# Spreading the second score product of a gated linear attention over four column quarters of TensorE

## Chip, core and metric

The kernel runs on one core of a Trainium2 chip. The metric is the device time of one launch in microseconds; the number given for a kernel is the median of its runs. Before the change it is 628.76 us (three runs, 627.93 to 629.44).

## What is computed

A gated recurrence over the sequence feeds a feed-forward block. For each of 4 batches and 8 heads (768 steps, 48 numbers per head) a complex state S is rotated and shrunk at each step by a gate (its size held below 0.999), takes up the outer product of k and v, and is read out by q:

```python
for t in range(S):
    ar, ai = a_re_n[:, :, t, :, None], a_im_n[:, :, t, :, None]
    new_re = ar * S_re - ai * S_im
    new_im = ar * S_im + ai * S_re
    S_re, S_im = new_re + einsum('bhd,bhe->bhde', k[:, :, t], v[:, :, t]), new_im
    y[:, :, t] = einsum('bhd,bhde->bhe', q[:, :, t], S_re)
x = y.transpose(0, 2, 1, 3).reshape(3072, 384)
h = maximum(maximum(x @ w1, x @ w2), x @ w3)        # 384 -> 768
out = h @ w_out                                      # 768 -> 384
```

All data are float32.

## The kernel before

**Tiles.** The sequence is cut into blocks of 128 steps. A group g is one block of two batches; each of its two halves (x and y in the step names, number x = 2g or 2g+1 in the code) is one block of one batch with 8 heads. There are 12 groups, so 24 halves. A block of 128 steps is two chunks of 64. Inside a chunk the recurrence is written as products: q and k are turned by the running angle of the gates and scaled by running products of their sizes, a masked score matrix (key step by query step) takes the place of the recurrence, and a state per head is carried from chunk to chunk.

**Scores.** In `scores` (L590) the step `A` (L602) multiplies K by Q for every head in pieces of 32 keys. Each product has 32 columns of weights, and its output lies in one of the four sets of 32 partitions (0, 32, 64, 96), which is one of the four column quarters of TensorE. In order, `A` walks over the four quarters for each head: 32 products a half, each with 80 columns of the moving operand. The steps `g0` to `g3` pick what is wanted out of A by masks into the tile `atm` (128 key steps, 8 heads, 64 query steps), on VectorE.

The second score product, step `B` (L608), covers the block of the first 32 keys against the last 32 queries of each chunk. It has a product for each head h and each chunk j: weights `KB` and moving operand `QB`, 32 columns each, 16 products a half. The output of chunk j lies at partition 64j, so the products use two of the four quarters, and column block h of one PSUM bank. Its results are carried to `atm` by `b0` and `b1` (L632), one ScalarE copy for each chunk: 32 partitions, 8 heads by 32 queries, from partitions 64j to the same partitions of `atm`. The step `y` (L678) then multiplies `v` and the carried state with `atm` and `QG`; its 56 products of 32 weight columns and 64 moving columns are spread over the four quarters by a round-robin over four queues.

**Feed-forward.** `xT` is a copy of y. The steps U (`up`, L710) make the three hidden products 128 by 128 by 256, u takes their maximum (`hT`), O and o make the output product (`op`) and its copy `ot`.

**What sets the order.** Every engine's order is written out by hand in two lists of step names: SCHEDULE (L21) for the opening, groups 0 and 1 and the preparation of the weights, and CYCLE (L52) for each later group. A small class (Bound, L122) ties each instruction to the one before it on its engine, so no scheduler moves anything; all instructions are issued from its line 131, so the profile shows L131 for all of them and they are told apart by the names of tiles. All PSUM tiles (`banks`, L141) rotate through four buffers of two banks each, so a fifth request waits until the first buffer has been read.

Each cycle of CYCLE has two B steps on TensorE: in one half the order is A, B, op, up, y, and in the other A, B, tp (a transpose of uq), op, y, tp.

Of the kernel before, what the change touches and what calls it, by code (L numbers as in the profile page):

```python
# [67 lines left out]
def kernel(  # L68
# [14 lines left out]
    B, H, S, D = q.shape  # L83
    P = 128
    L64 = 64
    DD = L64 + D
# [32 lines left out]
    T = {}  # L119
# [18 lines left out]
    pe, dve, act, pool, sp = (Bound(e) for e in (nc.tensor, nc.vector, nc.scalar, nc.gpsimd, nc.sync))  # L138
    mm = pe.matmul

    def banks(nm, n=None):  # L141

        ps = psum.tile([P, 2, 512], FP, tag="ps", name=nm)
        T["ps"] = ps
        return ps if n is None else ps.rearrange("p a n -> p (a n)")[:, 0:n]
# [61 lines left out]
    KB = const.tile([P, 2 * H, 32], FP, name="KB")  # L207
# [382 lines left out]
    def scores(x, name):  # L590

        atm = T["atm", x] = atms[x % 2]

        def pick(out, mask, data):
            dve.copy_predicated(out=out, mask=mask, data=data)

        def over(mask):

            n = mask.shape[-1]
            return mask.rearrange("p (b t) -> p b t", b=1).to_broadcast([P, H, n])  # L600

        if name == "A":  # L602
            ps = T["A", x] = banks("A")
            for h in range(H):
                for o in range(0, P, 32):
                    mm(out=ps[o:o + 32, h // HU, h % HU * P:h % HU * P + 80], lhsT=T["K", x][0:DD, h, o:o + 32],
                       rhs=T["Q", x][0:DD, 4 * h + o // 32], start=True, stop=True)
        elif name == "B":  # L608
            ps = T["B", x] = banks("B")
            for h in range(H):  # L610
                for j in range(2):
                    o = j * L64
                    mm(out=ps[o:o + 32, 0, h * 32:h * 32 + 32], lhsT=T["KB", x][0:DD, 2 * h + j],
                       rhs=T["QB", x][0:DD, 2 * h + j], start=True, stop=True)
        elif name[0] == "g" and name[1:].isdigit():
            src = T["A", x].rearrange("p a (b t) -> p (a b) t", b=HU)

            def own(lo, n):

                return src[:, :, lo:lo + n].rearrange("p h (j t) -> p h j t", j=1).to_broadcast([P, H, 2, n])  # L620

            i = int(name[1:])
            if i == 0:
                pick(atm.rearrange("p h (j t) -> p h j t", j=2), over(maskd).rearrange("p h (j t) -> p h j t", j=2),
                     own(0, 32))
            elif i == 1:
                pick(atm.rearrange("p h (j n u w) -> p h j n u w", j=2, n=2, u=2)[:, :, :, :, 1],
                     over(masko[:, 0]).rearrange("p h (j n w) -> p h j n w", j=2, n=2), own(48, 16))
            else:
                pick(atm.rearrange("p h (j u w) -> p h j u w", j=2, u=2)[:, :, :, 1],  # L630
                     over(masko[:, i - 1]).rearrange("p h (j w) -> p h j w", j=2), own(32 * (i - 1), 16))
        elif name in ("b0", "b1"):  # L632
            o = int(name[1]) * L64
            src = T["B", x][:, 0, 0:H * 32].rearrange("p (h t) -> p h t", h=H)
            act.copy(out=atm[o:o + 32, :, 32:], in_=src[o:o + 32])
        else:
            return False
        return True
# [106 lines left out]
    def run(name, g):  # L745
# [9 lines left out]
        elif name == "Zf":  # L755
            for t in fs:
                dve.memset(t[L64 // 2:L64], 0.0)
        elif name == "Zg":
            for t in gs:
                dve.memset(t[:, :, :, D:P - D], 0.0)  # L760
        elif name[0] == "W":
            i = int(name[2:])
            weight_load(i) if name[1] == "L" else weight_step(i, name[1])
        elif name[0] in "Uu" and name[1:].isdigit():
            up(2 * g + 1, TG, int(name[1]), int(name[2]), name[0].upper() if name[0] == "U" else "u")
        elif name[0] in "Uu" and name[1:3].isdigit():
            up(2 * g + "xy".index(name[3]), P, int(name[1]), int(name[2]), name[0])
        elif name[-1] in "01" and gates(g, [int(name[-1])], name[:-1]):
            pass
        elif gates(g, list(range(C)), name):  # L770
            pass
        else:
            c = "xy".index(name[-1])
            x, name = g * C + c, name[:-1]
            if name in ("Lr", "Li"):
                load_a(g, c, *(("ar", a_re) if name == "Lr" else ("ai", a_im)))
            elif name in ("Lk", "Lq"):
                load_kq(g, c, *(("k", k) if name == "Lk" else ("q", q)))
            elif name == "Lv":
                load_v(g, c)  # L780
            else:
                assert angles(g, c, name) or turns(g, c, name) or factors(x, name) or scores(x, name) \
                    or state(x, name) or outputs(x, name) or project(x, name), name
# [51 lines left out]
```

## Time and profile before

| what | before |
|---|---|
| median of runs | 628.76 us |
| the profiled execution's own time | 627.78 us |
| its span, first to last instruction | 625.9 us |
| mean granted TensorE clock | 0.986 |
| matmul instructions of B / A / y | 768 / 1536 / 2560 |
| ScalarE copies atm<-B | 48, 356 ns each |

A product of float32 is recorded as two weight loads and two matmuls, so the 16 products of one B step are 32 instructions of each kind. In the tables PE is TensorE's matmuls, PEld its weight loads, ACT ScalarE, DVE VectorE. "Busy" of PE counts matmuls that overlap in the array and whose ends are modelled; what a step costs is better read from where the next one starts. The chain of work gives the sequence of instructions that the end of the kernel depended on. An engine's idle time is noted with what released it.

### The profile page before, as it was taken

What the parts mean: (1) busy time and instruction counts of PE and PEld (TensorE: products, weight loads), DVE (VectorE), ACT (ScalarE), POOL (GpSimd) and SP (SyncE); (2) the same over time, 40 slices, a digit from 0 to 9 for tenths busy, and PEclk for the clock granted to TensorE, in tenths of its full rate; (3) what the DMA queues carried; (4) which work ended last, traced back from release to release, by engine and by line L of the source; (5) the groups of instructions that cost most, each with busy time, mean ns of one, the idle gap of its engine ahead of it and who ended that gap; (6) DMA issues with size and microseconds to landing.
All of it is one profiled execution on the core that took longest, in us unless ns stands there. A gap on an engine that the chain in (4) does not pass through costs nothing.

```text
span 625.9 us, 22651 instructions
## 1 busy us (share of the span) xinstructions
PE 588.8 (94%) x10124; PEld 473.1 (76%) x10124; DVE 478.7 (76%) x694; ACT 429.2 (69%) x698; POOL 14.3 (2%) x47
## 2 busy tenths in 40 slices
PE   4466899899999999999999999999999999999997
PEld 1255797688787787787788788788788788788785
DVE  6998999989887887877777787887887887754211
ACT  8998998795894894894894894894894893541100
POOL 3500000000000000000000000000000000000000
PEclk9976999999999999999999999999999999999999
DMA  9788411442222223122222222222230221000000
GB/s 241 171 210 209 115 20 35 93 80 43 50 57 51 51 56 72 27 60 52 50 56 52 53 54 52 53 52 52 53 66 15 41 53 28 15 3 15 15 13 25
DMA packets 136545, 39.24 MB, mean 63 GB/s; under 512 B 129153, under 2 KB 132225, under 8 KB 136449
## 3 DMA queue, kind: packets, MB, share of 16 engines
q1 hardware_dynamic: 136448, 37.80, 27.3%
q8 instruction: 79, 1.29, 0.9%
q14 instruction: 18, 0.14, 0.1%
HBM read 33.03 MB, written 4.72 MB: 60 GB/s over the span
## 4 chain that ended last, share of the span: by engine, by line
PE 84%; ACT 6%; DVE 5%; DMA 3%; issue 1%; SPq 1%; DVEq 0%; ACTq 0%
PE up L131 43%; PE op L131 16%; PE y L131 6%; PE A L131 4%; PE tp L131 4%; PE dk L131 3%; PE cs L131 2%; PE sums L131 2%; PE B L131 2%; DVE ex L131 2%; DVE w L131 2%; PE F L131 1%; DMA ai<-in_a_im_dram 1%; DMA raw<-in_moe_w_out_dram 1%; ACT L L131 1%
## 5 line engine op out<-in xcount | busy, mean ns | idle before, releaser
L131 PE MATMUL up<-xT,w 128*128 128x256 f32 (+1 forms) x1404 | 297.4, 368 | 2.2 <-ACT E L131 0.7
L131 PEld LDWEIGHTS up<-xT,w 128*128 128x128 f32 x1404 | 248.5, 191 | 39.8 <-ACT L L131 1.7
L131 DVE TENSOR_TENSOR hT<-hT,up 128x768 f32<-128x768 f32 (+1 forms) x56 | 46.8, 837 | 80.1 <-PE up L131 80.1
L131 PE MATMUL op<-wo,hT 128*128 128x384 f32 x288 | 98.8, 494 | 0.0
L131 PEld LDWEIGHTS op<-wo,hT 128*128 128x128 f32 x288 | 53.0, 190 | 33.4
L131 DVE TENSOR_TENSOR Q<-Q,f 112x512 f32<-112x512 f32 (+2 forms) x72 | 68.6, 953 | 9.6 <-ACT Q L131 9.2
L131 ACT ACT_TABLE_LOAD x47 | 60.3, 1283 | 1.6 <-PEq L819 0.8
L131 ACT COPY xT<-y 128x384 f32<-128x384 f32 x24 | 11.4, 476 | 62.6 <-PE y L131 62.6
L131 PE MATMUL y<-atm,vb 128*32 128x64 f32 x1152 | 39.9, 225 | 3.8 <-issue 3.0
L131 PEld LDWEIGHTS y<-atm,vb 128*32 128x32 f32 x1152 | 32.9, 112 | 13.7 <-issue 7.4
L131 ACT ACTIVATE f<-F 48x280 f32<-48x280 f32 x96 | 38.2, 398 | 2.5 <-PE F L131 1.2
L131 ACT ACTIVATE t<-cs 128x384 f32<-128x384 f32 x24 | 11.8, 491 | 39.8 <-PE cs L131 39.8
L131 PE MATMUL y<-QG,g 112*32 112x64 f32 x1408 | 38.8, 221 | 0.0
L131 PE MATMUL A<-Q,K 112*32 112x80 f32 x1536 | 32.6, 239 | 3.1 <-ACT w L131 2.6
L131 PEld LDWEIGHTS y<-QG,g 112*32 112x32 f32 x1408 | 35.3, 111 | 0.3 <-DVE g L131 0.2
L131 PEld LDWEIGHTS A<-Q,K 112*32 112x32 f32 x1536 | 28.1, 112 | 7.8 <-ACT e L131 2.7
L131 ACT COPY Q<-tp 112x1024 f32<-112x1024 f32 x24 | 24.3, 1011 | 12.7 <-PE tp L131 12.4
L131 DVE COPY_PREDICATED atm<-masko,A 128x256 f32<-128x256 uint8 x72 | 31.3, 435 | 1.5
L131 ACT COPY atm<-B 32x256 f32<-32x256 f32 x48 | 17.1, 356 | 19.0 <-DVE atm L131 18.7
L131 DVE TENSOR_TENSOR uk<-uk,En 128x768 f32<-128x768 f32 x24 | 22.9, 955 | 8.6 <-PE tp L131 8.5
L131 DVE TENSOR_TENSOR g<-g,dk 112x384 f32<-112x384 f32 x40 | 22.0, 550 | 9.7 <-PE dk L131 9.3
L131 PEld LDWEIGHTS dk<-vb,uk 64*48 64x48 f32 (+1 forms) x1408 | 23.1, 128 | 7.8 <-ACT K L131 2.6
(106 smaller groups left out, 886.6 us busy)
## 6 DMA issues: line engine op xcount, KB each, us to landing
ar<-in_a_re_dram SPq DMA_DIRECT2D x24, 192.0 KB
ai<-in_a_im_dram SPq DMA_DIRECT2D x24, 192.0 KB
q<-in_q_dram SPq DMA_DIRECT2D x96, 48.0 KB
k<-in_k_dram SPq DMA_DIRECT2D x96, 48.0 KB
vb<-in_v_dram SPq DMA_DIRECT2D x96, 48.0 KB
out_dram<-ot SPq DMA_DIRECT2D x24, 192.0 KB
raw<-in_moe_w_dram SPq DMA_DIRECT2D x5, 768.0 KB
w<-in_moe_w_dram SPq DMA_DIRECT2D x2, 768.0 KB
```

The lines of the kernel that those rows point to most:

```text
L131: ins = f(*a, **kw)
```

## The change

B takes its 16 products in another order and puts them elsewhere. For i in 0 to 3 and chunk j the heads i and 4 + i follow one another: heads 0 to 3 go to partitions 64j, heads 4 to 7 to partitions 64j + 32, both in column block i. So four successive products lie in four different quarters, and the result takes 128 partitions by 128 columns instead of twice 32 partitions by 256 columns. Number and shape of the products stay.

Each of b0 and b1 becomes two ScalarE copies of 32 partitions by 4 heads by 32 queries. The one of heads 0 to 3 reads the partitions that it writes; the one of heads 4 to 7 reads partitions 64j + 32 and writes partitions 64j. The contents of `atm` are the same. No other step changes, and the order of steps on each engine stays.

```diff
         elif name == "B":
             ps = T["B", x] = banks("B")
-            for h in range(H):
+            for i in range(4):
                 for j in range(2):
-                    o = j * L64
-                    mm(out=ps[o:o + 32, 0, h * 32:h * 32 + 32], lhsT=T["KB", x][0:DD, 2 * h + j],
-                       rhs=T["QB", x][0:DD, 2 * h + j], start=True, stop=True)
+                    for c in range(2):
+                        o, h = j * L64 + 32 * c, 4 * c + i
+                        mm(out=ps[o:o + 32, 0, i * 32:i * 32 + 32], lhsT=T["KB", x][0:DD, 2 * h + j],
+                           rhs=T["QB", x][0:DD, 2 * h + j], start=True, stop=True)
...
         elif name in ("b0", "b1"):
             o = int(name[1]) * L64
-            src = T["B", x][:, 0, 0:H * 32].rearrange("p (h t) -> p h t", h=H)
-            act.copy(out=atm[o:o + 32, :, 32:], in_=src[o:o + 32])
+            src = T["B", x][:, 0, 0:4 * 32].rearrange("p (h t) -> p h t", h=4)
+            for c in range(2):
+                act.copy(out=atm[o:o + 32, 4 * c:4 * c + 4, 32:], in_=src[o + 32 * c:o + 32 * c + 32])
```

## Prediction, made before the changed kernel ran

> **What bounds the kernel now.** I read the page's busy shares first, then the chain of work, then the chain inside one cycle, the rows of B by form, and last the starts of single instructions in the timeline.
>
> The page (line, column: engine and share of the chain that ended last):
>
> ```profile
> ## 4 chain that ended last, share of the span: by engine, by line
> PE 84%; ACT 6%; DVE 5%; DMA 3%; issue 1%; SPq 1%; DVEq 0%; ACTq 0%
> ```
>
> ACT is 69% busy and DVE 76%; the chain is TensorE's. Busy time by stretch shows where that holds (0 to 125 us is the opening, 125 to 580 the cycles, then the tail):
>
> ```profile
> 0.00:125.00 125.00, 93.05 (x1768) 72.11 (x1770) 116.30 (x190) 111.13 (x189) 14.35 (x47) 0.93 0.57 137
> 125.00:580.00 455.00, 454.01 (x8059) 369.14 (x8056) 355.39 (x496) 313.47 (x501) 0.00 (x0) 1.00 0.23 47
> ```
>
> The columns are PE, PEld, DVE, ACT, POOL, then the granted clock. In the cycles PE has work 454.0 of 455 us at full clock, DVE 355, ACT 313. In the opening DVE (116) and ACT (111 of 125) are the full ones. So time taken off TensorE counts in the cycles and mostly does not in the opening. One half of a cycle in the chain of work (start, us, what):
>
> ```profile
> 394.72 1.24 PE A L131 x64
> 395.96 0.50 PE B L131 x32
> 396.46 0.59 PE tp L131 x16
> 397.05 4.07 PE op L131 x12
> 401.12 1.72 PE y L131 x112
> 402.84 0.59 PE tp L131 x16
> ```
>
> No link is a wait. A: 64 matmuls of 80 columns in 1.24 us, 19 ns each. B: 32 of 32 columns in 0.50, 15.6 ns each: 2.5 times fewer columns, hardly faster. The rows by form:
>
> ```profile
> L131 PE MATMUL A<-Q,K 112*32 112x80 f32 x1536 | 32.6, 239 | 3.1 <-ACT w L131 2.6 <-DVE Q L131 0.5
> L131 PE MATMUL B<-QB,KB 112*32 112x32 f32 x768 | 16.4, 196 | 2.1 <-ACT f L131 2.1
> L131 ACT COPY atm<-B 32x256 f32<-32x256 f32 x48 | 17.1, 356 | 19.0 <-DVE atm L131 18.7
> ```
>
> **What holds B.** The timeline gives start times. In steady A four matmuls start 7 ns apart, then 49 ns pass: 69 ns for four. [...] In y (64 columns) four take 55 to 60. In B the starts are 13 and 19 ns apart in turn: two matmuls, one in each quarter, per 32 ns. [...] F, with 48 weight columns on a two by two division of the array, repeats every 45 ns; dk, with up to 64 weight columns on the same division, every 58.5 (start to start of four). 32, 48 and 64 weight columns against 32, 45 and 58.5 ns lie on a line: columns/1.2 plus 5. [...]
>
> [...]
>
> **TensorE's gain.** B issues 32 matmuls a half. Before: 16 groups of two, 16 x 32 = 512 ns, and 0.1 us until the next step starts (B at 395.78, tp at 396.39: 0.61). After, four neighbours lie in four quarters, as in A: 8 groups x 32 = 256 ns, and the same 0.1. The last members of a group start up to 20 instead of 13 ns after the first, so I take 0.25 us for a step of B.
>
> [...]
>
> What no row shows is four quarters that load and stream without a pause. The densest are A, 4 x (32 + 80) columns in 69 ns, 6.5 per ns, and y, 4 x (32 + 64) in 58, 6.6; B would need 4 x (32 + 32) in 32, 8 per ns. Issue is no nearer: pairs of load and matmul start 6.7 ns apart in the opening of A, 27 ns for four, against 32. Bounds of a group of four: 32 ns (saves 0.25), 39 at 6.6 columns/ns (saves 0.20), 45 as F (saves 0.15), 64 for no gain. [...]
>
> **Where it counts.** 20 of the 24 B steps start after 141 us. In all but the first of these, TensorE follows on without a wait, so 19 x 0.25 = 4.75 us. The four of the opening start at 49.5, 75.3, 105.3 and 117.5; the chain there is ACT or DVE for the first two (no gain), and PE with B in it (0.63 each) for the last two: 2 x 0.25 = 0.5.
>
> **ScalarE's cost.** 48 copies of 256 numbers become 96 of 128. Copies of 384 numbers take 476 ns, of 1024 1007: 0.83 ns a number, so a copy of 256 (356) has 143 fixed, and one of 128 takes 250. At most it is 356 (nothing saved by halving), at least 178 (nothing fixed). A half has then 4 x 0.25 + gaps of 12 ns = 1.04 instead of 0.72: 0.32 more (up to 0.70). Reading other partitions than are written needs no extra: of the 96 activations f<-F half move by 64 partitions, and all lie between 385 and 403 ns.
>
> [...] Behind the copies on ACT are queued, in one half, L, Q and xT, and xT waits 1.2 us for y; in the other xT, with a wait of 4.8. Who waits for the copies is y: they end at 399.69 and y starts at 401.05, cover 1.36; in the other half 378.25 and 381.23, cover 2.97. TensorE comes 0.25 earlier and the copies end 0.32 later, so 0.79 is left in the tighter half; even at 0.356 a copy 0.41 is left. Q to DVE then comes 0.3 later, before a DVE wait of 0.6 for tp. The next tight place, dk waiting for the copy of K (ends 411.06, dk 411.42, cover 0.36), is unmoved, since ACT before it and TensorE both start from y's end. QB is ready 0.5 before B, with A between. The PSUM buffer of B is asked for again by tp at 402.77, 3 us after its copies.
>
> The cover is missing in two places. At 51.16 to 51.89 the chain goes through both copies, and at 146.61 to 147.34, where y starts at 147.38. Each costs 0.32 (0.70 at most): 0.64. The first y of the cycles is the B step that I left out of the 19.
>
> **Sum.** Against the profiled execution's 627.78 us (span 625.9 and 1.9 around it): -4.75 - 0.5 + 0.64 = -4.6, so 623.2. The median before is 0.98 higher, so 624.2 as a median. With groups of 39 to 45 ns the 21 steps save 4.2 to 3.2 and the sum is -3.6 to -2.6; with copies of 0.356 it is -3.85.
>
> **Rivals.**
> - *Four quarters share a path.* 39 to 45 ns a group: 625.2 to 626.2. For it: 8 columns/ns is nowhere in the trace. [...] Chance 0.12.
> - *Nothing gained on TensorE.* If 16 ns a matmul is a floor of issuing or loading, not of a quarter, B stays at 0.50 and only the two bare places cost: 629.4, no measurable change. For it: 15.6 ns in B and 15.4 in y look alike. [...] Chance 0.07.
> - *Copies reach y (slower).* If a quarter copy that crosses partitions costs as much as two of today's, 0.71 us, a half has 2.13 us more, y of the tight half starts 0.77 later than now, 10 x 0.77 = 7.7, with 2 x 2.13 in the bare places, less 2.3 for nine halves with enough cover and 0.5: +9, 638. It turns slower from 0.52 us a copy. For it: ACT carries 12% more instructions in the cycles. Against it: the rows of f<-F. Chance 0.04, with 0.02 for slower in ways that I do not see.
>
> **How the numbers follow.** The full gain has 0.75: 624.2, own range 623.2 to 625.2 (runs before spread by 0.8 up and down). The range reaches down to 622.6, twice that spread below 624.2, and up to 626.8 for the shared path (626.2 and most of the spread). What a measurement here can tell from no change is about 0.2%, 1.3 us; full gain and shared path (0.87) lie beyond that. I give faster 0.86, same 0.08, slower 0.06.
>
> **What would show it.** In the changed profile B in the chain of work should stand at 0.25 us for 32 matmuls instead of 0.50, with starts in fours; the next step should start 0.36 us after B's first matmul, not 0.61. ACT's atm<-B should be x96 at about 250 ns, ACT's busy time up by 7 to 8 us, and y's idle before it should still be no wait for ACT. Wrong would be: B at 0.4 or more; copies above 0.36; a new wait of y or dk for ACT that takes back what B gave.

## The result and the profile after

The changed kernel takes 625.91 us (median of six runs, 624.75 to 627.30) against 629.13 us (six runs) for the kernel before; the ratio is 0.9947 with a 95% interval of 0.9930 to 0.9964, so 2.3 to 4.4 us less. In a later comparison, with five runs against nine, it is 625.78 against 630.09, ratio 0.9934 (0.9922 to 0.9947). The forecast was 4.6 less, 624.2, with a range of 622.6 to 626.8.

The profiled execution took 624.75 us, with a span of 622.9. Its busy time by stretch, columns as before (PE, PEld, DVE, ACT, POOL, granted clock):

```profile
0.00:125.00 125.00, 91.44 (x1744) 70.66 (x1744) 115.17 (x188) 112.46 (x196) 14.14 (x47) 0.89 0.56 136
125.00:580.00 455.00, 453.57 (x8119) 367.53 (x8120) 359.06 (x503) 320.16 (x542) 0.00 (x0) 1.00 0.23 47
```

TensorE still has no free time in the cycles, though B got shorter and ACT has 542 instructions there instead of 501. The same half of a cycle in the chain of work:

```profile
393.52 1.24 PE A L131 x64
394.77 0.29 PE B L131 x30
395.06 0.59 PE tp L131 x14
395.65 4.07 PE op L131 x12
399.72 1.73 PE y L131 x112
401.45 0.59 PE tp L131 x16
```

Every other link has its length of before; B's went from 0.50 to 0.29, not to 0.25. (The chain counts only the matmuls that lie on it, 30 of 32.) The rows by form:

```profile
L131 PE MATMUL B<-QB,KB 112*32 112x32 f32 x768 | 11.4, 198 | 1.4 <-ACT f L131 1.4
L131 ACT COPY atm<-B 32x128 f32<-32x128 f32 x96 | 24.4, 254 | 19.9 <-DVE atm L131 18.7
```

A copy of half the size takes 254 ns, where 250 was forecast, and ACT's busy time rose from 429.2 to 437.3 us.

From B's first matmul to the next step's first it is 0.41 us (0.407 to 0.409) in all halves of the cycles but one (0.388), against 0.611 before: 0.203 less, where I had counted 0.25. Over the cycles this adds up: from the A that starts at 160.81 before and 161.72 after, to the last y of the kernel (its last matmul, not its first), 425.57 us have become 421.64, so 3.93 less, which is 19 times 0.207. The start times of single matmuls show where 0.05 of each step stayed. For the half above, in ns from one start to the next:

```
B after:  7 7 6 9 6 7 7 11 7 7 6 12 7 6 7 12 6 7 7 11 7 7 6 12 | 12 16 4 13 17 16 17
```

Up to the bar it is as foreseen: four starts 7 ns apart, and a group of four every 32 ns. The last eight matmuls start 4 to 17 ns apart and no longer in fours. This loss, 0.04 to 0.05 us, is called the slow spot below.

The opening hides a part of the gain in this execution. Its sixth B starts at 162.85, before at 161.94, and the lag of 0.5 is there at the first B already, ahead of anything that the change touches. The last experiment shows it to be mostly scatter of the opening from one execution to another; the profiled execution of the kernel before, at 627.78, was faster than all of its timed runs.

### The profile page after: what moved, and what is told of

Its sections match the earlier page's. It is cut to its first block, busy times and chain, and to the rows that moved or that the text cites. A ratio compares the mean times of both kernels' runs of the same rounds, so it can differ in the third digit from the quotient of the medians.

```text
span 622.9 us, 22703 instructions
## 1 busy us (share of the span) xinstructions
PE 583.8 (94%) x10124; PEld 467.9 (75%) x10124; DVE 478.9 (77%) x694; ACT 437.3 (70%) x746; POOL 14.1 (2%) x47
## 4 chain that ended last, share of the span: by engine, by line
PE 84%; ACT 7%; SPq 4%; DVE 3%; issue 1%; DMA 0%; DVEq 0%; ACTq 0%
PE up L131 44%; PE op L131 15%; PE y L131 6%; SPq L131 4%; PE A L131 4%; PE tp L131 4%; PE dk L131 3%; PE cs L131 2%; PE sums L131 2%; PE F L131 1%; ACT L131 1%; PE B L131 1%; DVE Q L131 1%; ACT L L131 1%; PE pw L131 1%
## 5 line engine op out<-in xcount | busy, mean ns | idle before, releaser
L131 ACT COPY atm<-B 32x128 f32<-32x128 f32 x96 | 24.4, 254 | 19.9 <-DVE atm L131 18.7
L131 ACT COPY ot<-op 128x384 f32<-128x384 f32 x24 | 11.5, 478 | 25.5 <-PE op L131 25.4
```

Of the source, the lines that this page charges most:

```text
L131: ins = f(*a, **kw)
```

## Experiments

**Twice the products.** What makes the last eight matmuls slow? In this kernel B issues all its products a second time, into a bank that nobody reads. Theory S says that instructions come too slowly, theory T that the next step is to blame.

```diff
-            for i in range(4):
-                for j in range(2):
-                    for c in range(2):
+            for bank in range(2):
+                for i in range(4):
+                    for j in range(2):
+                        for c in range(2):
...
-                        mm(out=ps[o:o + 32, 0, i * 32:i * 32 + 32], lhsT=T["KB", x][0:DD, 2 * h + j],
+                            mm(out=ps[o:o + 32, bank, i * 32:i * 32 + 32], lhsT=T["KB", x][0:DD, 2 * h + j],
...
```

> The changed kernel with all 16 products of B issued a second time, into the other bank of B's PSUM tile, where nobody reads them. In the changed kernel the first 24 matmuls of B start 8 ns apart and the last 8 about 15 ns, and a step takes 0.41 us from its first matmul to the next step's first. Theory S (supply): instructions reach TensorE at no more than one pair of load and matmul per 16 to 17 ns, and B lives on a stock of about a dozen pairs; then everything after the 24th matmul runs at 16 to 17 ns, the step takes about 0.41 + 32 x 0.0165 = 0.94 us, and the kernel about 11 us more than the changed one (637). Theory T (tail): the last 8 are slow because the next step, in another division of the array, is at hand; then only the last 8 of 64 are slow, the step takes 0.41 + 0.256 = 0.67 us, and the kernel 5.4 us more (631).

639.46 us (one run). The timeline of one half (start, us, engine, count):

```profile
164.53 1.31 PE L131 MATMUL A<-Q,K 112*32 112x80 f32 x64
165.66 0.77 PE L131 MATMUL B<-QB,KB 112*32 112x32 f32 x64
166.39 0.66 PE L131 MATMUL tp<-ident,uq 64*112 64x64 f32 x16
```

The typical step takes 0.70 us, so 32 more matmuls cost 0.29, 9 ns each. Theory S as I put it, a supply of one pair in 16 to 17 ns, is wrong. So is T, though its 0.67 us comes near 0.70: the slow spot is still at the 25th matmul, and 39 more of B follow in the same division. After the spot, which costs about 0.05 us, the starts come as 15 and 2 in turn: two together every 17 ns, four in 33. The place of the spot depends on what came ahead of B: behind A it is the 25th matmul, and in the first three halves of the opening, where B had waited, the 33rd.

The kernel lost 13.5 us, more than 24 times 0.29 (7 us). In five places TensorE stands still, and no semaphore holds it. One of them, in the middle of a step:

```profile
237.05 0.60 PE L131 MATMUL B<-QB,KB 112*32 112x32 f32 x45
238.86 0.38 PE L131 MATMUL B<-QB,KB 112*32 112x32 f32 x19 [1.21 <-issue]
239.17 0.59 PE L131 MATMUL op<-wo,hT 128*128 128x384 f32 x1
```

"issue" says that no semaphore ended these 1.21 us. The others are 0.91, 1.06, 0.99 and, within op, 0.43 us. The cycles take 433.07 us instead of 421.64: 19 times 0.29 is half of this, and the five stops are most of the rest. The two executions of the changed kernel and that of the kernel before show none in the cycles.

The traces point to what the stops are. They name one DMA queue an instruction queue (packets, MB, share of 16 engines; first the changed kernel, then this one):

```profile
q8 instruction: 79, 1.29, 0.9%
q8 instruction: 85, 1.39, 0.9%
```

Each packet has 16384 bytes. This kernel has 1536 TensorE instructions more (768 loads, 768 matmuls) and six packets more, so by these counts the queue serves TensorE, and a packet goes with 256 of its instructions (an estimate, 1536 / 6). Counted through the trace, the five stops come after 8129, 9921, 11713, 15297 and 17089 recorded instructions of TensorE, and three stops in kernels further down each after 12481: every one is 193 above a multiple of 256. I call these places the ends of blocks. At the end of block 31, where the stop above is, packet 31 had ended 0.13 us before TensorE's last start, and TensorE went on 1.53 us after it. In all eight the packet of the same number ends between 0.38 us before the last start and 0.06 after it, and TensorE goes on 1.2 to 1.5 us after the packet's end. In the cycles of the kernel before and in both profiles of the changed kernel TensorE comes to the end of a block 2.0 us or more after its packet ended (3.8 or more in the first profile of the changed kernel, 4.5 before), and doesn't stop. So I take the stops for waits for instructions, an inference from these counts and times: no run moved a packet, and why these packets came late stays open.

**The copies alone.**

```diff
-            act.copy(out=atm[o:o + 32, :, 32:], in_=src[o:o + 32])
+            for c in range(2):
+                act.copy(out=atm[o:o + 32, 4 * c:4 * c + 4, 32:], in_=src[o:o + 32, 4 * c:4 * c + 4])
```

> The kernel before with b0 and b1 split into two copies of 4 heads each, all in the partitions of before; B stays in two quarters. My prediction: a pair of copies costs 0.16 us more, hidden in the cycles, and bare at two places (the first half of the opening and the first of the cycles), together +0.64 us on the kernel before (about 629.8). Theory O: the opening pays more than two places, as the changed kernel's profile stands 0.9 us behind at its sixth B; then +0.9 or more, with that lag in this profile too. Rival: the lag is an accident of that execution, and the copies cost under 0.3 us. If nothing were hidden: 24 x 0.33 = +8 us.

629.53 against 629.74 us, ratio 0.9996 (0.9987 to 1.0005): from 0.8 less to 0.3 more. The cycles are untouched: from the A near 161 us to the last y it is 425.50 us, before 425.57. 48 more copies cost nothing that can be measured here. At the two bare places that I had counted, y starts 0.05 and 0.06 us sooner after B than in the kernel before, not 0.32 later each. But this test is milder than I had meant. The four copies of one half in this kernel, and then in the changed kernel, in the timeline of ACT:

```profile
148.64 0.82 ACT L131 COPY atm<-B 32x128 f32<-32x128 f32 x4
```

```profile
147.42 1.06 ACT L131 COPY atm<-B 32x128 f32<-32x128 f32 x4
```

In the first, the two copies of a pair, which read the same partitions, start 0.15 to 0.17 apart and so overlap; from one pair to the next, where the partitions read are others, it is 0.26. In the changed kernel every copy reads other partitions than the one before it, and the starts are 0.25 to 0.28 apart. One alone takes 250 and 254 ns. So this run adds 0.1 us of copies to a half and the changed kernel 0.34, and two thirds of the cost are not tested by it. For it there is the changed kernel's own trace, whose cycles show no wait of y for a copy but the one foreseen, at 148 us.

**B ahead of A, in one half or in both.** Only the order lists change, and VectorE's QB in the second of the two kernels:

```diff
-sbx:1 sax:1 nfy:1 h1y:0 Q1y:0 Eky:1 Q3y:0 Eny:1 h2y:0 Dy:-2 Fx:1 f0x:1 U12:-1 h3y:0 Eqy:1 uqx:1 u12:-1 Ay:0
-add:2 f3x:1 g0y:0 g1y:0 By:0 g2y:0 f1x:1 f2x:1 lnL:2 g3y:0 QGy:0 expw:2 tpqx:1 expe:2 b0y:0 b1y:0 Oy:-1 ukx:1
+sbx:1 sax:1 nfy:1 h1y:0 Q1y:0 Eky:1 Q3y:0 Eny:1 h2y:0 Dy:-2 Fx:1 f0x:1 U12:-1 h3y:0 Eqy:1 uqx:1 u12:-1 By:0 Ay:0
+add:2 f3x:1 g0y:0 g1y:0 g2y:0 f1x:1 f2x:1 lnL:2 g3y:0 QGy:0 expw:2 tpqx:1 expe:2 b0y:0 b1y:0 Oy:-1 ukx:1
```

and in the second kernel also

```diff
-uqy:0 KBx:0 f1y:0 h1x:0 h2x:0 mky:0 Enx:1 U01:-1 f3y:0 Ekx:1 mulai:1 h3x:0 f2y:0 f0y:0 Eqx:1 uky:0 mulw:1
-sign:1 tpqy:0 Qcy:0 tpky:0 u01:-1 QBx:0 Lkx:1 stt:1 Ax:0 Bx:0 h0y:0 Kcy:0 g0x:0 sqr:2 atan:1 g1x:0 QBy:0
+uqy:0 KBx:0 QBx:0 f1y:0 h1x:0 h2x:0 mky:0 Enx:1 U01:-1 f3y:0 Ekx:1 mulai:1 h3x:0 f2y:0 f0y:0 Eqx:1 uky:0 mulw:1
+sign:1 tpqy:0 Qcy:0 tpky:0 u01:-1 Lkx:1 stt:1 Bx:0 Ax:0 h0y:0 Kcy:0 g0x:0 sqr:2 atan:1 g1x:0 QBy:0
```

> The changed kernel with B ahead of A, not behind it, in the y half of each cycle (11 of the 24 steps). By theory S the queue is full when B starts, since the step before it is up with 227 ns a matmul, and A after it takes 17 ns a pair, no more than the supply; so B to A should take 0.26 to 0.3 us (no slow tail), A's length should stay within 0.03 of 1.13, and A and B together should shrink by 0.05 us a half: 0.5 us in all, at the edge of what can be measured. By theory T the tail goes as well, since A has B's division of the array. If the slow tail belongs to B's own last products, nothing changes.

> The same in both halves of each cycle, with the VectorE step that makes QB in the x half moved ahead to follow KB, so that B doesn't wait for it. If e3 gains, this gains twice that: 20 x 0.05 = 1.0 us below the changed kernel (about 624.9). Rival: QB ahead of the steps for the state delays dk or g, and TensorE waits for VectorE: no gain or slower than e3.

626.21 us, ratio to the kernel before 0.9952 (0.9937 to 0.9968), and 626.62, ratio 0.9960 (0.9947 to 0.9973). Neither beats the changed kernel (0.9947, later 0.9934). The timeline of the second:

```profile
255.80 0.46 PE L131 MATMUL B<-QB,KB 112*32 112x32 f32 x32
256.07 1.34 PE L131 MATMUL A<-Q,K 112*32 112x80 f32 x64
257.34 0.66 PE L131 MATMUL tp<-ident,uq 64*112 64x64 f32 x16
```

B takes 0.27 to A, without a slow spot: all its 32 matmuls come in fours. So the spot is not tied to B's last products. But A now takes 1.265 instead of 1.131, and both together 1.539 us in either order. A's starts are 9 17 17 30 28 16 17 8 ns apart from its first matmul on, which is the 33rd counted from B's first; its rate stays at 69 ns for four, but the four quarters are out of step to the end, and the loss stands at the end. My expectation that A would hide it was wrong. From the first of A and B to the last y the cycles of the second kernel take 421.88 us, 0.24 more than those of the changed one; this is one half (B at 325.41) in which A starts that much later, by the profile after VectorE's hT. So the gain does not show, and no delay by the rival's dk or g shows either. The cycles of the first take 422.94 us, with one stop of 1.36, up to 373.35, at the end of a block.

**The same four quarters, other neighbours.**

```diff
-            for i in range(4):
-                for j in range(2):
-                    for c in range(2):
+            for c in range(2):
+                for i in range(4):
+                    for j in range(2):
```

> The changed kernel with c as the outermost loop: all four quarters are used, the same outputs lie in the same places, but neighbours in the stream alternate between two quarters (0 and 2, then 1 and 3). My theory: a place in the array needs 32 ns from one matmul to its next, and TensorE takes its instructions in order, so only neighbours in different quarters overlap: a step of B takes 0.61 us again, as in the kernel before, and the kernel stays at about 629.5. Rival: the four quarters alone do it, whatever the order (instructions pulled ahead over neighbours): 0.41 us.

629.6 us (one run), against 630.09 for the kernel before. That the time comes out as I had put it is chance: from first to last instruction this run has 626.4 us, 1.8 less than the 628.2 of the kernel before's median run, and the time around them was 3.2 us where it is 1.8 or 1.9 in most runs. The timeline:

```profile
255.67 1.31 PE L131 MATMUL A<-Q,K 112*32 112x80 f32 x64
256.80 0.59 PE L131 MATMUL B<-QB,KB 112*32 112x32 f32 x32
257.31 0.66 PE L131 MATMUL tp<-ident,uq 64*112 64x64 f32 x16
```

The step takes 0.518 us, neither 0.61 nor 0.41. The neighbours matter: at the beginning and at the end of the step two matmuls start per 32 ns, as in the kernel before. In the middle, about where c changes, three groups of four appear in 32 ns each (starts 6 7 6 13, 18 9 5 1, 17 8 5 2), and three times 32 is the 0.094 by which 0.518 falls short of 0.612. The records don't name a matmul's quarter, but one quarter gives a start every 32 ns, so four starts in 32 ns need all four. The first group of four comes after 9 or 10 matmuls, and 16 stand ahead of those for the other two quarters: so in this run matmuls for free quarters start ahead of about six for busy ones (an estimate, 16 less 10). In these starts TensorE isn't as strictly in order as I had put it, but it reached over no more than that. This profile also has one stop of 1.01 us, up to 374.38, at the end of a block; without it the cycles would take 424.0 us, 1.6 below the kernel before, for 19 x 0.094 = 1.8.

**A and B mixed.** After every 8 products of A, 4 of B (one per quarter), with PSUM tiles for both asked for at the start. Groups 0 and 1 stay unmixed; the order lists are those of the kernel with B first in both halves:

```diff
-        if name == "A":
...
-        elif name == "B":
...
+        if name in ("A", "B"):
...
+                parts = ["A", "A", "B"] * 4 if name == "A" else []
+            for nm in sorted(set(parts), reverse=True):
+                T[nm, x] = banks(nm)
...
```

> The kernel with B ahead of A in the cycles, but the two mixed: after every 8 products of A, 4 of B (one per quarter), A first. Both products then last 27 + 16 x 69 + 8 x 32 + 100 = 1.49 us if no start is lost; apart and in either order they take 1.54. Theory of the stock: about 32 pairs of load and matmul wait ready after a slow step, and where B runs through them at 8 ns a pair the four quarters get out of step by some 50 ns once; mixed, a group of 12 pairs takes 170 ns, 14 a pair, slower than the supply seen in e1 after its slow spot (8.5 a pair), so nothing is lost: 1.49, and 19 x 0.05 = 1 us less than the changed kernel. Rival: the 50 ns are lost at the 33rd pair whatever runs there: 1.54, no gain.

626.77 us, ratio 0.9950 (0.9936 to 0.9964). The timeline of one half:

```profile
257.22 0.48 PE L131 MATMUL A<-Q,K 112*32 112x80 f32 x16
257.52 0.24 PE L131 MATMUL B<-QB,KB 112*32 112x32 f32 x8
257.58 0.46 PE L131 MATMUL A<-Q,K 112*32 112x80 f32 x16
...
258.54 0.24 PE L131 MATMUL B<-QB,KB 112*32 112x32 f32 x8
258.71 0.66 PE L131 MATMUL tp<-ident,uq 64*112 64x64 f32 x16
```

From 257.22 to 258.71 it is 1.495 us, as worked out, and all starts come in fours. So the 50 ns are not lost at the 33rd pair as such; they are lost where B's products follow one another with no A between them. The kernel as a whole is not faster for it: the cycles of its profile take 422.34 us, with one stop of 1.40 us before op, up to 375.54, at the end of a block: the load of the weights has started and only the matmul is missing. Without this stop they would be 420.9, 0.7 below the changed kernel's 421.64. Whether such stops explain the medians of these kernels can't be told from one profile each.

**The changed kernel again.**

> The changed kernel once more, to be compared on this chip with the others and with the kernel before. From its first six runs 3.2 us below the kernel before; from the trace, 19 to 20 steps at 0.20 us give 3.9 less what the opening takes. If the opening's lag of 0.9 us in its first profile is an accident, this profile's first B steps stand within about 1 us of those of the kernel before on either side, and the kernel is 3.2 to 4 us faster; if it is of the change, they stand 0.6 to 1 us later again.

625.78 us, ratio 0.9934 (0.9922 to 0.9947). In this profile the first six B steps stand 1.2 to 1.9 us later than in the kernel before's, and the cycles take 421.69 us, within 0.05 of the first. The opening's lag has grown by 0.7 between two executions of one kernel. In the copies-only kernel it was 0.56 at the first B, -0.10 at the third and 1.96 at the sixth. So the lag is mostly scatter; what the change does to the opening is better read step by step, as in the next section.

## Why the prediction was right, and where its terms were off

- **The bound.** TensorE sets the pace of the cycles and nothing hides its time: shown. All of the 0.203 us that a step lost is found again in the length of the cycles (3.93 us).
- **32 ns per place, four places side by side.** Shown for the first 24 matmuls of the step in 19 of the 20 halves from 141 us on, 8 columns/ns included: groups of four every 32 ns. In the other half, the one of 0.388 us, the first slip comes after the fifth matmul (30 ns to the next). The rival of a shared path, 39 to 45 ns a group, is out. The 0.25 us a step of the sum takes it that four places load and stream each for itself; no run shows that as such. What the runs show in its place is the starts, two in 32 ns in B before and four in 32 ns after, and 0.203 us less a step. One of the points behind the working is softer than it looked: of dk's 1408 loads half have 64 columns and half 48.
- **0.25 us a step.** Too high by 0.05, and this is the largest miss. My 8 x 32 + 100 ns is 0.356; measured is 0.408. I had set issue aside because pairs start 6.7 ns apart in A's opening; the pace of 8 ns held here for 24 matmuls behind A, and for 32 after a wait. The spot at the 25th or 33rd pair and its absence where A and B are mixed speak for a stock of up to 32 pairs, an estimate from these places alone. But with B doubled four matmuls start every 33 ns after the spot; a supply that near to the pace of 32 would hardly empty a stock in 32 pairs. So the cause of the spot is not shown, nor why it is the 25th pair behind A.
- **19 steps, and two of the opening.** The 19 give 3.93. The two of the opening, forecast at 0.25 each, gave next to nothing: from B's first matmul to the next step's first it was 0.693 us at the third B and 0.643 at the fourth, and it is 0.695 and 0.631 in both executions of the changed kernel. At the third the next step, dk, now waits for ScalarE's f (0.24 us in the first profile). I had taken the chain through TensorE there as it stood, and not asked what would end next behind it.
- **The copies.** 250 ns forecast, 254 measured; ACT 7 to 8 us more forecast, 8.1 measured; all hidden in the cycles. At the bare y of 148 us I had 0.32 and it was 0.05: the wait before y went from 0.885 to 1.142, and 0.203 of this is B's. The reason is in the instructions: y's first matmuls wait for the third copy only, and a later one for the fourth, so y started at 148.24 while the last copy ran (147.42 to 148.48). At 51 us it is the same: the copies took 1.08 instead of 0.73, but y came only 0.06 later after B's start (2.52 instead of 2.46). So the bare places cost 0.11 together, not 0.64.
- **The sum.** -4.75 - 0.5 + 0.64 = -4.6 becomes -3.93 - 0.01 + 0.11 = -3.8. The medians say -3.2 (2.3 to 4.4 less) and, the second time, -4.3 (3.3 to 4.9). That the opening's gain and the bare copies, both far too large in my sum, nearly cancel was luck. The first median, 625.91, lies above the range that I gave for the full gain (623.2 to 625.2) and among the times that I gave for the shared path (625.2 to 626.2); it is the starts, not the time, that tell the two apart.
- **Rivals.** "Nothing gained on TensorE" and "copies reach y" are both out: the one by 0.408, the other by the missing wait.

The chance for the full gain leaned on a step of the working that I had no row for, a long run of pairs at 8 ns. I named 8 columns/ns as the unseen thing; it held, and the starts gave way after 24 matmuls, for a reason that no run here shows.

## What to carry to other kernels

Where products are small, read the start times and not the mean duration: the repeat of two starts in 32 ns pointed to one place in the array as the limit, and the four starts in 32 ns after the change showed that other places were free. Let neighbours in the program lie in different quarters: here the step took 0.41 us so, 0.52 with the same quarters in another order, and 0.61 with two quarters. When a stretch gets several times denser in instructions, ask how long it keeps the pace of a short burst: starts 8 ns apart held here for 24 to 32 matmuls. And where TensorE stops without a semaphore, count its instructions up to the stop: here all eight such stops in the cycles lay a multiple of 256 apart.

## Not expected of the hardware

- Matmuls in one place of the array repeated every 32 ns in B and every 45 in F, with 32 and 48 weight columns, and every 58.5 in dk, where half of the loads have 64 and half 48; with 32 columns, four places together gave four starts in 32 ns for the first 24 to 32 matmuls.
- After 24 pairs at 8 ns (32 in the opening with B doubled), the four quarters fell out of step once, as the starts show it, and stayed so until the step ended (0.05 us, in 19 of the 20 halves from 141 us on).
- The kernels with denser or reordered products show single stops of TensorE of 0.4 to 1.4 us that no semaphore ends (for op in two of them the profile names ACT's e, done 0.6 us earlier): five with B doubled, one each in three others, none in two executions of the changed kernel. All eight lie at the end of a block of 256 instructions, and end 1.2 to 1.5 us after an instruction packet did.
- Two copies on ACT that read the same partitions started 0.15 to 0.17 us apart, and 0.25 to 0.28 where the second reads others, though each takes 250 ns.
